# Row 0 of w3 and half of w_out loaded in fp32 on SP and cast on chip, q of batch 0 on POOL's queue, all queues listed anew

## The chip, the cores and the metric

The kernel runs on one core of one Trainium2 chip. The metric is device time in microseconds: the median of several executions. Five engines run their own instruction queues: TensorE (PE: matmuls and transposes; PEld is its loading of weights), VectorE (DVE), ScalarE (ACT), GpSimd (POOL) and SyncE (SP). Here POOL and SP also issue the transfers between memory and the chip; 16 DMA engines carry them. Transfers issued by POOL can change the type on the way (fp32 in memory, fp16 on chip); those that SP issues copy as they are.

## The reference, cut to what matters

```python
# q, k, v: (8, 8, 576, 64); w1, w2: (512, 1024); w3: (1024, 1024); w_out: (1024, 512), all fp32
q_s = softmax(q, over the 64 features); k_s = softmax(k, over the 576 positions)
kv  = einsum('bhsd,bhse->bhde', k_s, v)
x   = einsum('bhsd,bhde->bhse', q_s, kv)      # laid out as 4608 tokens x 512
h   = (x @ w1) * (x @ w2) @ w3
out = h @ w_out                               # 4608 x 512
```

## The kernel before, in words

The two last products are folded: W3O = w3 @ w_out is made once (1024 x 512), and each token needs only x @ w1, x @ w2, their product elementwise, and one product with W3O. All matmuls take fp16 operands.

The work is cut into named steps. A step's name holds its kind, batch or chunk, and part. A class `Plan` (L19 on) takes every step with its engine, what it needs and what it frees; the order in which the steps are emitted is not computed but written out in one long text, `ORDER`. Each engine gets its instructions in that order and runs them strictly one behind the other; semaphores make a step wait for what it needs. `PICKS` says which engine does a step that more than one engine could do (evictions from the matmul banks above all). The lists `HW`, `LOADS` and `LATE` give the transfers: `HW` and `LATE` go to SP's queue, `LOADS` to POOL's, each in the order of its list (L436 to L441). A load on POOL's queue also waits until the load eight before it has landed. `FILL` puts empty matmuls (L362, on a tile of zeros) into TensorE's queue at the start and ahead of a named step.

The steps that the prediction speaks of:

- `w3.r` loads rows of w3: r = 0 to 3 are one block of 128 rows each, `w3.4` holds blocks 4 and 5, `w3.5` blocks 6 and 7. `wo.0` and `wo.1` load the halves of w_out. `w1.c`, `w2.c` load a quarter of the columns of w1 and w2. `q.0.p`, `k.b`, `v.b` load q, k, v; q of batches 0 and 1 comes in two parts, p = 0 of 1024 and p = 1 of 1280 elements on each of 128 partitions.
- Folding, for each block ft of w3 (L453 to L484): `w3t.ft` transposes it on TensorE (eight 128x128 transposes, L457), `w3T.ft` copies it out on ACT or DVE, `pf.ft.0` and `pf.ft.1` multiply it with the two halves of w_out (four matmuls each, L469), `W3O.ft` copies the result out with a scale.
- q of batch b, part p: `qmx` (largest of 64, DVE, L640), `qsub` (DVE or POOL, L645), `qexp` (ACT, L653), `qsm` (sum, DVE, L658), `qeps`, `qrc` (reciprocal), `qn` (product, POOL, L677). For batch 0 `qt.0.n` then transposes it on TensorE (L692), and `qT` copies that out.
- k of batch 0: `kmx.0.0` (four operations on DVE, L510 to L513), `kT`, `kr`, `kB` (largest over all positions, by TensorE and DVE, L547 to L559), `ksub`, `kexp`; `kv.0` multiplies with v (L603, L613), `kv2` scales, `xm` and `xt` make x (L725).
- Chunk c of tokens: `up.1.c.s.u` is the product with w2, `up.0.c.s.u` that with w1 (L857), `bs` copies the first out, `ab` multiplies the two on DVE (L872), `down` is the product with W3O (L879, L894 for the last chunk), `os` copies it out and `st` stores it.

Before, `HW` is the two parts of q of batch 0, and `LOADS` begins with w3.4, w3.0, wo.0, wo.1, k.0, w3.3, w3.2, w3.5, v.0, k.1, q.1.0, w2.0, w1.0, w3.1, w2.1, w1.1. The fold starts with block 4.

Of the kernel before, what the change touches and what calls it, by code (L numbers as in the profile page):

```python
# [82 lines left out]
W3O.2 w3T.6 w3T.7 kve.0 k.2 pf.7.0 w2.2 pf.6.0 kv2.0 xm.0.0 w1.2 kmx.1.0 qmx.1.0 cba.1 xs.0.0.0 w2.3
qsub.1.0 xs.0.0.1 w1.3 pf.6.1 pf.7.1 xm.0.1 xs.0.1.1 xs.0.1.0 W3O.7 up.1.0.0.0 up.0.0.0.0 bs.0.0.0
cbx.1 ab.0.0.0 cb.1 xt.0 up.1.0.1.0 bs.0.1.0 W3O.6 v.1 w3t.1 w3T.1 ksub.1.1 q.1.1 up.0.0.1.0
up.1.0.0.1 ab.0.1.0 pf.1.0 up.0.0.0.1 qexp.1.0 xts.0.0 xts.0.1 bs.0.0.1 qsm.1.0 ab.0.0.1 up.1.0.1.1
up.0.0.1.1 pf.1.1 kexp.1.1 kmx.2.0 qeps.1.0 W3O.1 bs.0.1.1 up.1.0.0.2 up.0.0.0.2 up.1.0.1.2 qrc.1.0
ab.0.1.1 bs.0.0.2 cba.2 cbx.2 ab.0.0.2 up.0.0.1.2 bs.0.1.2 ab.0.1.2 ksub.1.0 q.2 up.1.0.0.3
up.0.0.0.3 up.1.0.1.3 up.0.0.1.3 cb.2 bs.0.0.3 kexp.1.0 qn.1.0 ksub.2.1 ab.0.0.3 down.0.0 ksub.2.0
vc.1.1 vc.1.0 qmx.1.1 os.0.0 bs.0.1.3 kv.1 kve.1 ab.0.1.3 kv2.1 qmx.2.1 qsub.1.1 down.0.1 down.0.2  # L90
qd.1.0 kexp.2.0 os.0.1 kexp.2.1 qexp.1.1 xm.1.0 down.0.3 xs.1.0.0 xs.1.0.1 qmx.2.0 qsub.2.1 qsub.2.0
qsm.1.1 qeps.1.1 os.0.2 qrc.1.1 qexp.2.1 qexp.2.0 qn.1.1 v.2 k.3 q.3 up.1.1.0.0 up.0.1.0.0 bs.1.0.0
up.1.1.0.1 up.0.1.0.1 ab.1.0.0 st.0.0 vc.2.0 bs.1.0.1 qd.1.1 qsm.2.1 qeps.2.1 os.0.3 ab.1.0.1 st.0.3
st.0.1 qrc.2.1 qn.2.1 qsm.2.0 qd.2.1 vc.2.1 qeps.2.0 up.1.1.0.2 up.0.1.0.2 up.1.1.0.3 up.0.1.0.3
qrc.2.0 qn.2.0 qd.2.0 bs.1.0.2 ab.1.0.2 bs.1.0.3 kv.2 kve.2 ab.1.0.3 down.1.0 kv2.2 qmx.3.1 xm.1.1
down.1.1 xs.1.1.0 xs.1.1.1 xt.1 os.1.0 kmx.3.0 xts.1.0 xts.1.1 cba.3 qmx.3.0 up.1.1.1.0 up.0.1.1.0
up.1.1.1.1 up.0.1.1.1 bs.1.1.0 qsub.3.1 qsub.3.0 bs.1.1.1 xm.2.0 cbx.3 ab.1.1.0 xs.2.0.0 cb.3
xs.2.0.1 qexp.3.1 up.1.1.1.2 up.0.1.1.2 xm.2.1 xs.2.1.1 bs.1.1.2 ab.1.1.1 ab.1.1.2 xs.2.1.0
up.1.1.1.3 up.0.1.1.3 up.1.2.0.0 bs.1.1.3 qsm.3.1 ksub.3.0 q.4 ab.1.1.3 bs.2.0.0 qexp.3.0 qmx.4.1
ksub.3.1 up.0.2.0.0 up.1.2.0.1 up.0.2.0.1 up.1.2.0.2 bs.2.0.1 ab.2.0.0 qsm.3.0 up.0.2.0.2 up.1.2.0.3  # L100
ab.2.0.1 up.0.2.0.3 kexp.3.0 qeps.3.0 qrc.3.0 qsub.4.1 bs.2.0.2 up.1.2.0.4 qeps.3.1 qn.3.0 kexp.3.1
ab.2.0.2 qrc.3.1 qn.3.1 st.0.2 k.4 v.4 v.3 q.5 vc.3.1 qmx.4.0 kmx.4.1 qsub.4.0 bs.2.0.3 down.1.2
up.0.2.0.4 vc.3.0 os.1.1 os.1.2 up.1.2.0.5 qexp.4.1 bs.2.0.4 bs.2.0.5 kv.3 ab.2.0.3 kmx.4.0 ab.2.0.4
down.1.3 qd.3.0 qmx.5.1 qd.3.1 qexp.4.0 os.1.3 kve.3 kv2.3 vc.4.1 vc.4.0 qsub.5.1 up.0.2.0.5
ab.2.0.5 up.1.2.0.6 up.0.2.0.6 xm.3.1 bs.2.0.6 xm.3.0 ab.2.0.6 xs.3.0.1 xs.3.1.0 xs.3.1.1 xs.3.0.0
xt.2 cba.4 qsm.4.0 cbx.4 up.1.2.0.7 up.0.2.0.7 bs.2.0.7 v.5 k.5 q.6 st.1.0 st.1.2 xts.2.0 qeps.4.0
up.1.3.0.0 up.0.3.0.0 cb.4 ab.2.0.7 bs.3.0.0 ab.3.0.0 xts.2.1 ksub.4.1 qsm.4.1 up.1.3.0.1 up.0.3.0.1
up.1.3.0.2 bs.3.0.1 up.0.3.0.2 up.1.3.0.3 ab.3.0.1 up.0.3.0.3 down.2.0 qeps.4.1 qmx.5.0 kmx.5.1
qrc.4.1 kexp.4.1 qexp.5.1 ksub.4.0 bs.3.0.2 kexp.4.0 qsub.5.0 qn.4.1 os.2.0 bs.3.0.3 vc.5.1 qexp.5.0
st.1.3 v.6 st.1.1 st.2.0 qd.4.1 kv.4 ab.3.0.2 kmx.5.0 up.1.3.0.4 up.0.3.0.4 qrc.4.0 qn.4.0 ab.3.0.3  # L110
up.1.3.0.5 up.0.3.0.5 qsm.5.1 qeps.5.1 cba.5 bs.3.0.4 vc.6.1 down.2.1 kve.4 qsm.5.0 vc.5.0 cbx.5
os.2.1 down.2.2 down.2.3 cb.5 ksub.5.0 bs.3.0.5 qd.4.0 ab.3.0.5 qrc.5.1 ab.3.0.4 up.1.3.0.6
up.0.3.0.6 kv2.4 os.2.2 os.2.3 qmx.6.1 bs.3.0.6 xm.4.1 xt.3 qeps.5.0 ab.3.0.6 qrc.5.0 xs.4.1.1
ksub.5.1 kexp.5.0 qn.5.0 xs.4.1.0 qmx.6.0 k.6 up.1.3.0.7 bs.3.0.7 up.0.3.0.7 ab.3.0.7 down.3.0
kmx.6.0 os.3.0 kmx.6.1 kexp.5.1 xts.3.0 xts.3.1 xm.4.0 xt.4 xts.4.1 kv.5 kve.5 xs.4.0.0 xts.4.0
xs.4.0.1 qn.5.1 cba.6 down.3.1 down.3.2 kv2.5 up.1.4.0.0 vc.6.0 bs.4.0.0 cbx.6 st.2.2 up.0.4.0.0
up.1.4.0.1 up.0.4.0.1 up.1.4.0.2 qd.5.0 st.2.1 qd.5.1 st.2.3 ab.4.0.0 qsub.6.1 bs.4.0.1 st.3.0 q.7
k.7 v.7 os.3.1 os.3.2 st.3.1 ab.4.0.1 cb.6 xm.5.1 xm.5.0 bs.4.0.2 xs.5.0.1 xs.5.0.0 xs.5.1.1
qexp.6.1 ksub.6.1 up.0.4.0.2 up.1.4.0.3 qsub.6.0 ab.4.0.2 up.0.4.0.3 up.1.4.0.4 bs.4.0.3 up.0.4.0.4
ksub.6.0 kexp.6.1 bs.4.0.4 qexp.6.0 xs.5.1.0 ab.4.0.3 up.1.4.0.5 ab.4.0.4 bs.4.0.5 up.0.4.0.5  # L120
up.1.4.0.6 qsm.6.1 ab.4.0.5 kexp.6.0 qeps.6.1 bs.4.0.6 up.0.4.0.6 up.1.4.0.7 qmx.7.1 up.0.4.0.7
up.1.5.0.0 bs.4.0.7 ab.4.0.7 qrc.6.1 ab.4.0.6 down.3.3 qn.6.1 down.4.0 vc.7.1 os.3.3 qsm.6.0
# [878 lines left out]
```

## Time and profile before

| | |
|---|---|
| median of 3 runs | 239.43 us (239.19 to 239.56) |
| the profiled execution | 239.15 us, its span 237.4 us |
| TensorE busy | 229.5 us, 97% of the span |
| VectorE busy | 172.7 us, 73% |
| ScalarE busy | 122.1 us, 51% |
| POOL busy | 115.5 us, 49% |
| moved by DMA | 46.84 MB, mean 197 GB/s |

The span runs from the first to the last instruction of the profile; some 1.75 us of the execution lie around it. Busy time does not tell what bounds a kernel. The prediction reads TensorE's idle time from its instructions in order of time, and what ended each wait. A row of a timeline has the start, the length, engine, line, operation, the tiles by name, and the count; in brackets stands the idle time before it and what ended it. Where several instructions of one kind follow each other they are one row, from the first start to the last end, so that rows of TensorE, whose matmuls are pipelined, overlap a little. Tile names: `w` is w3 on chip, `wosb` w_out, `w1sb` and `w2sb` the others, `en` the normalized q, `po` and `pab` matmul banks.

### The profile page before, as it was taken

To read this page: it belongs to the slowest core of one execution; us is meant where nothing else is said; L and a number is where in the kernel's file an instruction comes from. 1 tells how busy PE (TensorE), PEld (TensorE's weight loads), DVE (VectorE), ACT (ScalarE), POOL (GpSimd) and SP (SyncE) were. 2 spreads that over 40 slices of the span, in tenths; PEclk is the share of its full clock that TensorE was granted. 3 is DMA by queue.
4 is the path that set the end of the run, shared out by engine and by line. 5 is a ranking of instruction groups with operands and counts; after the bars stand their busy time and mean duration, and the time that the engine had idled before them with its cause. 6 is when DMAs were issued, how large, how long until landed. Compare 5 with 4: busy or idle time off the path is not lost.

```text
span 237.4 us, 4852 instructions
## 1 busy us (share of the span) xinstructions
PE 229.5 (97%) x1935; PEld 119.1 (50%) x1935; DVE 172.7 (73%) x263; ACT 122.1 (51%) x225; POOL 115.5 (49%) x75
## 2 busy tenths in 40 slices
...
GB/s 211 214 310 207 343 202 303 322 309 384 300 225 309 403 342 266 391 391 157 237 115 193 401 172 102 143 79 3 122 68 0 1 3 133 29 94 95 50 132 133
DMA packets 40038, 46.84 MB, mean 197 GB/s; under 512 B 18384, under 2 KB 24272, under 8 KB 40016
## 3 DMA queue, kind: packets, MB, share of 16 engines
...
q8 instruction: 15, 0.25, 0.4%
q14 instruction: 7, 0.06, 0.1%
...
## 4 chain that ended last, share of the span: by engine, by line
PE 90%; DMA 6%; DVE 1%; POOL 1%; issue 1%; ACT 0%; ACTq 0%; DVEq 0%; POOLq 0%
PE pab L857 53%; PE po L879 24%; DMA k<-in_k_dram 6%; PE po L469 4%; PE po L894 3%; PE pkv L603 2%; PE xm L725 1%; PE pab L725 1%; PE w3t L457 1%; PE po L725 1%; DVE kmx L510 1%; POOL wosb L416 0%; POOL w L416 0%; DVE kmx L511 0%; DVE w3T L335 0%
## 5 line engine op out<-in xcount | busy, mean ns | idle before, releaser
L872 DVE TENSOR_TENSOR ab<-pab,bsb 128x512 f16<-128x512 f32 x72 | 48.5, 682 | 29.8 <-PE pab L857 15.1
L857 PE MATMUL pab<-x,w2sb 128*128 128x512 f16 (+1 forms) x320 | 66.0, 337 | 0.0
L857 PE MATMUL pab<-x,w1sb 128*128 128x512 f16 (+1 forms) x320 | 65.9, 337 | 0.0
L879 PE MATMUL po<-W3O,ab 128*128 128x512 f16 x256 | 59.2, 379 | 0.0
L857 PEld LDWEIGHTS <-w1sb 128*128 128x128 f16 x352 | 34.0, 98 | 28.5 <-issue 0.8
L857 PEld LDWEIGHTS <-w2sb 128*128 128x128 f16 x352 | 33.6, 98 | 28.1 <-issue 1.1
L335 ACT CAST bsb<-pab 128x512 f16<-128x512 f32 x47 | 27.1, 586 | 27.2 <-PE pab L857 26.9
L677 POOL TENSOR_TENSOR en<-eq,qr 128x1280 f16<-128x1280 f16 (+1 forms) x15 | 32.8, 2196 | 17.0 <-ACT qr L664 10.0
L578 POOL TENSOR_TENSOR k<-k,cb 128x1152 f32<-128x1152 f32 x12 | 31.5, 2632 | 19.5 <-issue 10.0
L879 PEld LDWEIGHTS <-ab 128*128 128x128 f16 x256 | 24.5, 98 | 28.9 <-issue 0.4
L335 ACT COPY osb<-po 128x512 f32<-128x512 f32 (+1 forms) x26 | 14.9, 575 | 40.9 <-PE po L879 35.2
L645 POOL TENSOR_TENSOR q<-q,qm 128x1024 f32<-128x1024 f32 (+1 forms) x14 | 29.7, 2125 | 5.7 <-issue 4.0
L640 DVE TENSOR_REDUCE qm<-q 128x16 f32<-128x1024 f32 (+1 forms) x16 | 21.4, 1340 | 3.3 <-DMA q<-in_q_dram 3.3
L658 DVE TENSOR_REDUCE qr<-eq 128x20 f32<-128x1280 f16 (+1 forms) x16 | 21.4, 1336 | 1.7 <-ACT eq L653 1.7
L335 DVE CAST bsb<-pab 128x512 f16<-128x512 f32 x25 | 17.1, 683 | 7.6 <-PE pab L857 7.1
L586 ACT ACTIVATE ek<-k 128x1152 f16<-128x1152 f32 x16 | 18.6, 1163 | 6.9 <-DVE k L578 3.6
L653 ACT ACTIVATE eq<-q 128x1024 f16<-128x1024 f32 (+1 forms) x16 | 18.5, 1164 | 3.9 <-DVE q L645 3.0
L501 DVE TENSOR_REDUCE km<-k 128x128 f32<-128x1152 f32 x8 | 17.3, 2168 | 0.0
L469 PE MATMUL po<-wosb,w3T 128*128 128x512 f16 x64 | 15.5, 379 | 0.7 <-DMA wosb<-in_moe_w_out_dram 0.5
L335 DVE COPY osb<-po 128x512 f32<-128x512 f32 (+1 forms) x11 | 7.2, 664 | 5.9 <-PE po L894 5.6
L335 ACT CAST v<-v 128x1152 f16<-128x1152 f32 x9 | 10.3, 1156 | 1.8 <-DMA v<-in_v_dram 1.8
L469 PEld LDWEIGHTS <-w3T 128*128 128x128 f16 x64 | 5.8, 97 | 7.2 <-issue 0.9
...
## 6 DMA issues: line engine op xcount, KB each, us to landing
...
```

The lines of the kernel that those rows point to most:

```text
L335: return [(nc.scalar.copy if eng == "ACT" else engine[eng].tensor_copy)(out=out, in_=in_)]
L469: nc.tensor.matmul(st["pf", ft], lhsT=st["w3T", ft][:, gt, :], rhs=wosb[:, gt, :], start=(gt == 0), stop=(gt == N_FT - 1))
L578: return [engine[eng].tensor_tensor(out=kb[:, two(hp), :, :], in0=kb[:, two(hp), :, :], in1=st["cb", b][:, two(hp), None, :].broadcast_to( ...
L586: nc.scalar.activation(out=st["ek", b][:, hp, :, :].rearrange("p j (i d) -> p i j d", i=2), in_=kb[:, two(hp), :, :], func=AF.Exp)
L640: dve.tensor_reduce(out=st["qm", b][:, :, j], in_=qb[:, :, j, :], axis=AX.X, op=ALU.max)
L645: return [engine[eng].tensor_tensor(out=qb[:, :, j, :], in0=qb[:, :, j, :], in1=st["qm", b][:, :, j, None].broadcast_to([P, HH, n, D]), op ...
L653: nc.scalar.activation(out=st["eq", b, p], in_=qb[:, :, j, :], func=AF.Exp)
L658: dve.tensor_reduce(out=st["qr", b][:, :, slice(*PARTS[p])], in_=st["eq", b, p], axis=AX.X, op=ALU.add)
L677: return [engine[eng].tensor_tensor(out=st["en", b][:, j, :, :].rearrange("p j h d -> p h j d"), in0=st["eq", b, p], in1=st["qr", b][:, :, ...
L857: nc.tensor.matmul(st["p", one, c, sub, u][:, a * (t1 - t0):(a + 1) * (t1 - t0)], lhsT=w[:, ct, fb * P:(fb + 1) * P], rhs=x()[:, ct, t0:t1 ...
L872: dve.tensor_tensor(out=st["ab", c][:, nf * u:nf * u + nf, t0:t1], in0=cut(st["p", 0, c, sub, u]), in1=cut(st["bsb", c, sub, u]), op=ALU.mult)
L879: nc.tensor.matmul(st["po", c, tb], lhsT=st["ab", c][:, ft, tb * P:(tb + 1) * P], rhs=W3O[:, ft, :], start=(ft == 0), stop=(ft == N_FT - 1))
```

## The change

- `HW` becomes w3.0 and wo.1: SP loads the first block of w3 (512 KB) and the second half of w_out (1 MB) in fp32, into the buffers that q and v of batch 1 take later. New steps cast them to fp16, in pieces of 1024 elements for each partition: `cast.w3.0.0` and `cast.wo.1.0` on ACT, `cast.wo.1.1024` on VectorE. `w3t.0` needs the first, `pf.ft.1` the other two.
- Both parts of q of batch 0 move to the head of `LOADS`, on POOL's queue, the larger part first, then wo.0, w3.4, k.0, w3.3, w3.2, w3.1, w3.5, v.0, k.1, q.1.0, w2.0, w1.0, w1.1, w2.1. POOL makes the identity (`ident`) ahead of its first load.
- The fold starts with block 0. `FILL` goes from 17 fills at the start and 6 ahead of `pf.4.0` to 10 at the start and 16 ahead of `pf.0.0`.
- `ORDER`, `PICKS` and `LATE` are listed anew through the whole kernel. In batch 0, `qsub.0.0` goes from VectorE to POOL, `w3t.1` comes ahead of `kv.0` instead of between the first products of chunk 0, and `qt.0.0` stands right behind `kB.0`.

```diff
 ORDER = """
-q.0.0 qmx.0.0 qsub.0.0 qexp.0.0 q.0.1 qmx.0.1 w3.4 qsub.0.1 w3.0 wo.0 ident w3t.4 wo.1 k.0 qexp.0.1
-w3T.4 qsm.0.1 w3.3 w3.2 w3.5 v.0 w3t.0 w3t.5 w3T.0 qeps.0.1 qrc.0.1 ident32 pf.4.0 pf.0.0 pf.4.1
+w3.0 wo.1 ident cast.w3.0.0 w3t.0 w3T.0 cast.wo.1.1024 q.0.1 q.0.0 cast.wo.1.0 wo.0 w3.4 k.0 qmx.0.1
+qsub.0.1 w3.3 qmx.0.0 w3.2 pf.0.0 pf.0.1 w3t.5 qexp.0.1 ident32 qsm.0.1 qeps.0.1 qrc.0.1 w3.1 w3.5
+qsub.0.0 v.0 qn.0.1 k.1 qexp.0.0 w3t.4 w3T.5 pf.5.0 pf.5.1 w3T.4 W3O.0 qsm.0.0 qeps.0.0 qrc.0.0
+pf.4.0 pf.4.1 kmx.0.0 w3t.3 qt.0.16 W3O.5 w3T.3 q.1.0 w2.0 w1.0 w1.1 qn.0.0 w3t.2 qt.0.8 w2.1 W3O.4
+w3T.2 kT.0 kr.0 pf.3.0 kB.0 qT.0.16 qT.0.8 qt.0.0 qT.0.0 pf.2.0 pf.3.1 pf.2.1 w3t.6 w3t.1 w3t.7
...
 FILL = {
-    "begin": 17, "pf.4.0": 6,
+    "begin": 10, "pf.0.0": 16,
 }
...
 HW = [
-    ("q", 0, 0), ("q", 0, 1),
+    ("w3", 0), ("wo", 1),
 ]
...
 LOADS = [
-    ("w3", 4), ("w3", 0), ("wo", 0), ("wo", 1), ("k", 0), ("w3", 3), ("w3", 2), ("w3", 5), ("v",
-    0), ("k", 1), ("q", 1, 0), ("w2", 0), ("w1", 0), ("w3", 1), ("w2", 1), ("w1", 1), ("k", 2),
-    ("w2", 2), ("w1", 2), ("w2", 3), ("w1", 3), ("v", 1), ("q", 1, 1),
+    ("q", 0, 1), ("q", 0, 0), ("wo", 0), ("w3", 4), ("k", 0), ("w3", 3), ("w3", 2), ("w3", 1),
+    ("w3", 5), ("v", 0), ("k", 1), ("q", 1, 0), ("w2", 0), ("w1", 0), ("w1", 1), ("w2", 1),
+    ("k", 2), ("w2", 2), ("w1", 2), ("w2", 3), ("w1", 3), ("v", 1), ("q", 1, 1),
 ]
...
     def home(name):
-        x = RAW.index(name)
-        return [("v", 1), ("q", 1)][x // 2], slice(x % 2 * 1024, x % 2 * 1024 + 1024)
+        return {"wo": ("v", 1), "w3": ("q", 1)}[name[0]], 2048 if name[0] == "wo" else 1024
...
+    def pieces(name):
+        return [(x, x + 1024) for x in range(0, home(name)[1], 1024)]
+
+    def wt(n):
+        return [("cast", *n, x0) for x0, _ in pieces(n)] if n in RAW else [n]
...
     for name in RAW:
-        def cast(eng, name=name):
-            to = st["cast", name].rearrange("p a x -> p (a x)")
-            return copy(eng, to, raw(name))
-        plan.add(("cast", *name), {"DVE": (1.2, True), "ACT": (1.02, False)}, 0,
-                 cast, needs=[name], lead=60.0)
-    wt = lambda n: [("cast", *n) if n in RAW else n]
+        for x0, x1 in pieces(name):
+            def cast(eng, name=name, x0=x0, x1=x1):
+                to = st["cast", name].rearrange("p a x -> p (a x)")
+                return copy(eng, to[:, x0:x1], raw(name)[:, x0:x1])
+            plan.add(("cast", *name, x0), {"DVE": (1.2, True), "ACT": (1.02, False), "POOL": (1.15, True)}, 0,
+                     cast, needs=[name], lead=60.0)
```

More of the change, by code (lines that the diff above doesn't have):

```diff
@@ L83 @@
[L83 to L122, printed above, removed]
@@ new lines @@
+up.1.0.0.0 up.0.0.0.0 up.1.0.1.0 bs.0.0.0 cba.1 ab.0.0.0 bs.0.1.0 w2.3 w1.3 xt.0 up.0.0.1.0
+up.1.0.0.1 qsub.1.0 v.1 cbx.1 cb.1 up.0.0.0.1 ab.0.1.0 xts.0.1 qexp.1.0 qsm.1.0 bs.0.0.1 qeps.1.0
+q.1.1 ksub.1.1 pf.1.0 ab.0.0.1 W3O.6 kmx.2.0 qrc.1.0 kexp.1.1 up.1.0.1.1 pf.1.1 xts.0.0 bs.0.1.1
+W3O.1 cba.2 q.2 up.0.0.1.1 up.1.0.0.2 up.0.0.0.2 up.1.0.1.2 bs.0.0.2 ab.0.1.1 ab.0.0.2 bs.0.1.2
+ksub.1.0 cbx.2 cb.2 qn.1.0 qd.1.0 up.0.0.1.2 up.1.0.0.3 ab.0.1.2 up.0.0.0.3 up.1.0.1.3 up.0.0.1.3
+kexp.1.0 vc.1.1 vc.1.0 bs.0.0.3 ab.0.0.3 down.0.0 ksub.2.1 bs.0.1.3 kv.1 qmx.1.1 qsub.1.1 ab.0.1.3
@@ new lines @@
+os.0.0 down.0.1 down.0.2 kexp.2.1 kve.1 kv2.1 qmx.2.1 qexp.1.1 os.0.1 os.0.2 xm.1.0 xs.1.0.1
+ksub.2.0 xs.1.0.0 qsub.2.1 down.0.3 up.1.1.0.0 up.0.1.0.0 up.1.1.0.1 qmx.2.0 qsm.1.1 qsub.2.0
+qeps.1.1 qrc.1.1 qexp.2.1 qsm.2.1 qn.1.1 k.3 v.2 q.3 vc.2.0 bs.1.0.0 ab.1.0.0 bs.1.0.1 up.0.1.0.1
+up.1.1.0.2 up.0.1.0.2 up.1.1.0.3 qd.1.1 st.0.0 st.0.2 qexp.2.0 ab.1.0.1 kexp.2.0 qeps.2.1 qrc.2.1
+qsm.2.0 qn.2.1 qd.2.1 vc.2.1 bs.1.0.2 kv.2 qeps.2.0 ab.1.0.2 bs.1.0.3 up.0.1.0.3 qrc.2.0 qn.2.0
+ab.1.0.3 kve.2 os.0.3 kv2.2 qmx.3.1 down.1.0 kmx.3.0 cba.3 xm.1.1 xs.1.1.0 xs.1.1.1 qsub.3.1 qd.2.0
@@ new lines @@
+qmx.3.0 q.4 st.0.1 down.1.1 xt.1 up.1.1.1.0 up.0.1.1.0 os.1.0 os.1.1 xts.1.1 up.1.1.1.1 bs.1.1.0
+up.0.1.1.1 xts.1.0 ab.1.1.0 xm.2.0 cbx.3 xs.2.0.0 cb.3 xs.2.0.1 bs.1.1.1 qexp.3.1 ab.1.1.1
+up.1.1.1.2 up.0.1.1.2 bs.1.1.2 xm.2.1 up.1.1.1.3 up.0.1.1.3 xs.2.1.0 xs.2.1.1 ab.1.1.2 bs.1.1.3
+qsm.3.1 qsub.3.0 qexp.3.0 ksub.3.0 up.1.2.0.0 ksub.3.1 up.0.2.0.0 up.1.2.0.1 qsm.3.0 qeps.3.1
+qrc.3.1 qn.3.1 qeps.3.0 ab.1.1.3 qrc.3.0 qn.3.0 k.4 st.0.3 v.3 q.5 qd.3.1 bs.2.0.0 vc.3.1 kexp.3.1
+ab.2.0.0 kmx.4.0 bs.2.0.1 down.1.2 up.0.2.0.1 up.1.2.0.2 qmx.4.1 bs.2.0.2 kexp.3.0 os.1.2 up.0.2.0.2
@@ new lines @@
+up.0.3.0.7 bs.3.0.7 ab.3.0.7 down.3.0 qrc.5.0 k.6 st.2.1 down.3.1 kmx.6.1 kmx.6.0 v.6 cba.6 qd.5.1
+xs.4.0.0 xs.4.0.1 kexp.5.0 kexp.5.1 qn.5.0 os.3.0 qd.5.0 st.2.3 st.3.0 xt.4 kv.5 xts.4.0 xts.4.1
+cbx.6 vc.6.0 q.7 qmx.6.1 up.1.4.0.0 up.0.4.0.0 kve.5 bs.4.0.0 down.3.2 ab.4.0.0 kv2.5 qmx.6.0
+up.1.4.0.1 up.0.4.0.1 up.1.4.0.2 bs.4.0.1 os.3.1 st.3.1 v.7 st.2.2 os.3.2 ab.4.0.1 bs.4.0.2
+up.0.4.0.2 up.1.4.0.3 ab.4.0.2 bs.4.0.3 xm.5.1 xm.5.0 xs.5.1.1 xs.5.0.0 xs.5.0.1 xs.5.1.0 up.0.4.0.3
+up.1.4.0.4 up.0.4.0.4 up.1.4.0.5 ab.4.0.3 bs.4.0.4 up.0.4.0.5 up.1.4.0.6 ab.4.0.4 up.0.4.0.6 cb.6
@@ new lines @@
+qsub.6.1 qexp.6.1 qsub.6.0 vc.6.1 down.3.3 qsm.6.1 bs.4.0.5 qexp.6.0 qeps.6.1 ab.4.0.5 qmx.7.1
+ksub.6.0 bs.4.0.6 qsm.6.0 up.1.4.0.7 up.0.4.0.7 ab.4.0.6 bs.4.0.7 up.1.5.0.0 up.0.5.0.0 qeps.6.0
+ab.4.0.7 bs.5.0.0 up.1.5.0.1 up.0.5.0.1 qrc.6.1 qmx.7.0 ksub.6.1 kexp.6.1 kexp.6.0 qrc.6.0 ab.5.0.0
+up.1.5.0.2 up.0.5.0.2 k.7 kmx.7.1 bs.5.0.1 down.4.0 up.1.5.0.3 kv.6 qn.6.0 qsub.7.1 bs.5.0.2 st.3.2
+qd.6.0 qn.6.1 kmx.7.0 cba.7 ab.5.0.1 up.0.5.0.3 vc.7.1 qexp.7.1 os.3.3 os.4.0 cbx.7 vc.7.0 qd.6.1
+st.4.0 down.4.1 up.1.5.0.4 ab.5.0.2 bs.5.0.3 down.4.2 st.3.3 ab.5.0.3 cb.7 os.4.1 bs.5.0.4
```

79 lines of the change are left out of this document (46 added, 33 removed), and 111 rows, old and new, of the table PICKS.

## The prediction

> **What bounds the kernel now.** I read the stretches first, to learn where TensorE is not busy, then TensorE's instructions in order of time in the first 15 us, then the chain that ended last, and then the queues that feed those microseconds. The stretches (start:end, length, then busy microseconds of each engine with instruction counts, PE, PEld, DVE, ACT, POOL, then clock, DMA share and GB/s):
>
> ```profile
> 23.00:234.40 211.40, 211.31 (x1826) 109.99 (x1824) 158.60 (x241) 113.02 (x212) 100.53 (x53) 1.00 0.72 194
> 60.00:120.00 60.00, 59.94 (x576) 32.35 (x573) 55.50 (x82) 45.68 (x89) 50.14 (x26) 1.00 0.99 295
> ```
>
> From 23 us to its last matmul TensorE is busy 211.31 of 211.40 us. There is 0.1 us to win there, whatever is listed anew; there is more to lose, since VectorE is busy 55.50 of 60 us in the middle. So the time is decided by how much of its work TensorE has done by about 34 us. The start, in order of time (start, length, then what; in brackets the idle time before it):
>
> ```profile
> 1.55 5.66 PE L362 MATMUL po<-zero 128*128 128x512 f16 x17 [1.55 <-DVE zero L357]
> 8.64 0.70 PE L457 MATMUL w3t<-ident,w 128*128 128x128 f16 x8 [1.43 <-DMA w<-in_moe_w_dram]
> 9.93 1.20 PE L457 MATMUL w3t<-ident,w 128*128 128x128 f16 x16 [0.59 <-DMA w<-in_moe_w_dram]
> 10.97 1.46 PE L362 MATMUL po<-zero 128*128 128x512 f16 x6
> 12.48 1.89 PE L469 MATMUL po<-wosb,w3T 128*128 128x512 f16 x8
> 14.82 0.38 PE L469 MATMUL po<-wosb,w3T 128*128 128x512 f16 x1 [0.46 <-DMA wosb<-in_moe_w_out_dram]
> ```
>
> Here every step but the empty fills (L362) waits for a transfer. The landings are those of one stream: w3 rows 4 and 5 at 8.64, row 0 at about 9.9, the first half of w_out by 12.4, the second at 14.8. In source bytes, 2.62 MB in 6.18 us is 0.424 MB/us. Later, the chain that ended last (start, length, what):
>
> ```profile
> 22.42 0.59 PE kB L559 x8
> 23.01 0.65 PE w3t L457 x8
> 23.66 0.86 PE po L469 x4
> 24.52 0.45 PE qtp L692 x8
> 24.97 1.73 PE po L469 x8
> 26.69 0.49 PE w3t L457 x8
> 27.19 0.71 PE pkv L603 x72
> 27.89 0.54 PE pkv L613 x36
> 28.43 1.83 PE po L469 x8
> 30.26 0.34 PE xm L725 x8
> 30.60 1.83 PE po L469 x8
> 32.44 0.34 PE xm L725 x8
> 32.78 1.33 PE pab L857 x11
> ```
>
> TensorE is dense here. The first products with w2 start at 32.78, those with w1 eight matmuls later, at about 33.65. The queues (packets, MB, share of the engines, in the slice from 5 to 6 us; then single issues of 256 KB with their time to landing), and POOL's issues in order of time:
>
> ```profile
> q1 hardware_dynamic: 196, 0.23, 68.1%
> q0 software_dynamic: 47, 0.10, 50.7%
> ...
> w1sb<-in_moe_w_dram POOLq DMA_DIRECT2D x1, 256.0 KB, 15.5
> ...
> w<-in_moe_w_dram POOLq DMA_DIRECT2D x1, 256.0 KB, 15.5
> ```
> ```profile
> 13.46 2.34 POOL L677 TENSOR_TENSOR en<-eq,qr 128x1280 f16<-128x1280 f16 x1 [2.54 <-DVE qr L670]
> 15.75 0.81 POOL L416 DMA_DIRECT2D q<-in_q_dram  x1
> 16.55 0.76 POOL L416 DMA_DIRECT2D w2sb<-in_moe_w_dram  x1
> 18.05 0.74 POOL L416 DMA_DIRECT2D w1sb<-in_moe_w_dram  x1 [0.74 <-DMA k<-in_k_dram]
> 19.18 0.54 POOL L416 DMA_DIRECT2D w<-in_moe_w_dram  x1 [0.39 <-DMA w<-in_moe_w_dram]
> 20.42 0.74 POOL L416 DMA_DIRECT2D w2sb<-in_moe_w_dram  x1 [0.69 <-DMA w<-in_moe_w_dram]
> 21.18 1.92 POOL L677 TENSOR_TENSOR en<-eq,qr 128x1024 f16<-128x1024 f16 x1
> ```
>
> The first piece of w1, issued at 18.05, lands 15.5 us later, at 33.55, 0.1 us before its use. Row 1 of w3, queued behind it, lands at 19.18 + 15.5 = 34.68: 0.52 MB of source take 1.13 us. So the stream and TensorE finish the start together.
>
> **The change, part by part.** The bytes read do not change: fp32 is read from memory either way, and a casting transfer only writes half. So I order the transfers by source bytes and give each the landing of before at the same count.
>
> Weights on SP, q on POOL. SP's queue now carries 0.52 MB of w3 and 1.05 MB of w_out where it carried 1.18 MB of q. POOL makes the identity before its first transfer, about 0.65 us later than now; POOL's packets begin only in the slice from 5 to 6 us above, as SP's run out, so SP's 0.39 MB more cover that. If they did not, the whole stream would slip by up to 0.65 us. Row 0 of w3 lands as the first 0.52 MB of q do now. These rows are VectorE's (and one of ScalarE's):
>
> ```profile
> 4.56 1.22 DVE L640 TENSOR_REDUCE qm<-q 128x16 f32<-128x1024 f32 x1 [3.06 <-DMA q<-in_q_dram]
> 5.81 1.23 DVE L645 TENSOR_TENSOR q<-q,qm 128x1024 f32<-128x1024 f32 x1
> 6.95 1.48 DVE L640 TENSOR_REDUCE qm<-q 128x20 f32<-128x1280 f32 x1
> 8.46 1.49 DVE L645 TENSOR_TENSOR q<-q,qm 128x1280 f32<-128x1280 f32 x1
> 11.29 1.49 DVE L658 TENSOR_REDUCE qr<-eq 128x20 f32<-128x1280 f16 x1 [1.34 <-ACT eq L653]
> ```
> ```profile
> 9.99 1.27 ACT L653 ACTIVATE eq<-q 128x1280 f16<-128x1280 f32 x1 [1.86 <-DVE q L645]
> ```
>
> So row 0 is there at 4.56. ScalarE casts it in about 1 us (by its 1.27 us for 1280 elements), and TensorE transposes it at about 5.75, behind the ten fills that are left, 4 us sooner than now. That gains nothing: the next product, row 0 with w_out, needs the first half of w_out, which is third on POOL's queue. With 3.80 MB up to its end, as now, it lands at about 12.4. The 16 fills run from 6.3 to about 10 and cost nothing, because that wait covers them to 12.4. The other two casts (1 us on ScalarE, and 1.2 to 1.5 us on VectorE by the rows above) start when w_out's second half lands, at about 7.2; VectorE is done by 8.7, and then q arrives. Without that cover VectorE's cast would delay q by its own length.
>
> TensorE to 23 us. First product at 12.45, eight matmuls, 14.2. Rows 4 and 5 of w3 come at 4.85 MB, where w_out's second half was: 14.85. Sixteen transposes take 1.04 (9.93 to 10.97 above): 15.9. The copy of the first of them on VectorE ends at about 16.25, so 0.35 idle. From there to the end of kB stands the same work as now after 14.82: sixteen matmuls 3.46, two sets of transposes 1.04, ten of q 0.55, kT 0.44, four matmuls 0.87, kB 0.6, together 6.96. End at 23.2; now it is 22.42 + 0.59 = 23.0.
>
> q's chain. q's larger part lands at 2.23 MB, where rows 4 and 5 of w3 were: 8.65, about 2.4 us later than now. VectorE reduces it (1.48) and subtracts (1.49): 11.65; it reduces the smaller part (1.22): 12.85. The smaller subtraction moves to POOL: 1.92 by the row for that size, 14.75. Behind it wait, on POOL, the issue of v (0.77; its bytes are due only after 23 us, so no loss), the larger product (2.34; ScalarE 1.27, VectorE 1.49 and two small steps make its input ready at 15.1): 17.85; then five issues, 0.8 + 4 x 0.76, 21.7; then the smaller product (1.92): 23.6, against 23.1 now. Its transposes now stand right behind kB: 23.65, so 0.4 idle on TensorE. Their 0.45, twelve matmuls 2.6, and three sets of transposes 1.5 give 28.2; kv 1.25, eight matmuls 1.73, xm 0.34, eight matmuls 1.73, xm 0.34: the first product with w2 at 33.6. One of those three sets is row 1 of w3, which now comes after 33.65 and takes 0.49. On TensorE alone the change costs 33.6 - 32.78 - 0.49 = 0.33 us.
>
> The stream. Row 1 of w3 now goes ahead of the pieces of w1 and w2. So the first piece of w1 lands where row 1 did, at 34.68, and its product starts at 34.74 instead of 33.65; TensorE waits 0.27 us for it, behind 33.6 + 0.87. Less the 0.49 us done early: **+0.60 us**. The two costs are not added, since the wait contains the first.
>
> Bounds of the stream. The 1.57 MB on SP can move as q did there (1.18 MB by about 5.6 us, 0.39 MB/us) or as the weights do now (0.424): 0 to 0.3 us later; the 1.18 MB of q, now on POOL, may gain by the same two rates, up to 0.25 us. I take 0, between them; the ends are +0.35 and +0.9.
>
> The rest. The list moves about as many evictions to VectorE as from it and reorders later loads and stores. I cost it at nothing: the cover is that 211.31 of 211.40 us. If it fails, one reduction of 1.2 to 1.5 us ahead of a multiply on VectorE is the price each time.
>
> Sum: the profiled execution took 239.15 us, span 237.4. Plus 0.60 is 239.75. The median of the runs, 239.43, lies 0.28 higher; against it I forecast **240.0 us**, with 239.8 to 240.4 for this case alone.
>
> **The rivals.** About 0.2%, 0.48 us, is what a measurement of this kernel can tell from no change.
>
> *Nothing to measure.* The weights need no cast in the transfer, and the stream runs some 0.3 us earlier. Then w1 comes with TensorE's own path, and +0.3 is left: 239.7. For it: q's gain may be near its 0.25; against it: casting transfers read faster now than SP's q did, and less of them is left. That the change does not do what it says belongs here: the early fold of row 0 moves one transpose, and nothing behind it.
>
> *The array's clock drops.* The 17 fills take 5.66 us where eight matmuls of L469 take 1.73, so 17 should take 3.68: a slow start costs up to 1.98 us. After the fills TensorE is idle from about 10 to 12.4. If it starts slowly again there, the first eight matmuls end at 15.9 instead of 14.2, 1.05 beyond the wait that follows, and 0.25 falls behind it; the 0.4 us of q's wait vanish. The first product with w1 starts at 35.4: +1.3, 240.7. Against it: in the rows above there is no untransposed matmul from 7.21 to 10.97, and the six fills then take 1.46, which is 0.24 each.
>
> [...]
>
> *A new wait in the relisted rest*, with VectorE the bound between 60 and 120 us: +0.6 + 1.5, 241.5. For it: 55.50 of 60 busy; against it: the present list has the same load and no wait.
>
> *Faster.* The large rows of the fp32 weights move on SP so much faster that the stream leads by over 1.08 us; then both bounds lie below now, 0.33 - 1.08 on TensorE and 0.60 - 1.08 by w1; the later decides, -0.48: 238.95 and below. For the first 2.75 MB that needs 0.57 MB/us on SP, against 0.39 to 0.424 in any row above.
>
> **How the numbers follow.** Forecast 0.46, nothing to measure 0.26, clock 0.08, new wait 0.11, faster 0.09. The forecast's lower edge, 239.8, lies within 0.48 us of 239.43, so 0.06 of it counts as the same. Faster 0.09; same 0.26 + 0.06 = 0.32; slower 0.40 + 0.08 + 0.11 = 0.59. The range runs from 239.2, which leaves out faster, to 241.1, which takes in the clock and leaves out most of the new wait.
>
> **What would show it.** In the profile after: the transposes of row 0 near 5.75 us, the first product at 12.4 waiting for w_out, rows 4 and 5 at 14.85; transposes of q at 23.6 behind POOL's product; the first product with w1 near 34.7 with a wait for its transfer; no TensorE wait later, the last matmul near 235.0. First products of 0.43 us each would show the clock. A landing of w1 well before 34 us, or a TensorE wait after 36 us, would make the prediction wrong.

## The result and the profile after

The changed kernel takes **240.11 us** (median of 6 runs, 239.76 to 240.49), the kernel before 239.25 us beside it (239.00 to 239.56): a ratio of 1.0036, with a 95% interval from 1.0023 to 1.0049. The profiled execution took 240.19 us, its span 238.4 us.

First TensorE's instructions in order of time after the change (start, length, then what; in brackets the idle time before it):

```profile
1.55 4.45 PE L363 MATMUL po<-zero 128*128 128x512 f16 x10 [1.55 <-DVE zero L358]
5.79 0.72 PE L463 MATMUL w3t<-ident,w 128*128 128x128 f16 x8
6.35 3.62 PE L363 MATMUL po<-zero 128*128 128x512 f16 x16
12.56 3.40 PE L475 MATMUL po<-wosb,w3T 128*128 128x512 f16 x8 [2.60 <-DMA wosb<-in_moe_w_out_dram]
15.76 1.33 PE L463 MATMUL w3t<-ident,w 128*128 128x128 f16 x16
17.38 3.63 PE L475 MATMUL po<-wosb,w3T 128*128 128x512 f16 x16 [0.29 <-DVE w3T L336]
...
24.16 0.62 PE L698 MATMUL qtp<-ident,en 128*128 128x128 f16 x8
...
34.35 1.05 PE L863 MATMUL pab<-x,w2sb 128*128 128x256 f16 x8
35.23 1.04 PE L863 MATMUL pab<-x,w1sb 128*128 128x256 f16 x8
```

Row 0 of w3 is transposed at 5.79 and the first product starts at 12.56, as forecast. But its eight matmuls take 3.40 us, 0.43 each, where sixteen at 17.38 take 3.63. The transposes of rows 4 and 5 do not wait for their transfer any more; they wait for TensorE. The same stretch by time (start:end, length, busy time of PE, PEld, DVE, ACT, POOL, then the granted clock, DMA share, GB/s), and two stretches that cover the rest:

```profile
12.00:12.50 0.50, 0.00 (x0) 0.00 (x0) 0.50 (x1) 0.50 (x1) 0.00 (x0) 1.00 1.06 201
12.50:13.00 0.50, 0.44 (x2) 0.27 (x3) 0.36 (x1) 0.50 (x2) 0.06 (x1) 0.77 1.10 209
13.00:16.00 3.00, 3.00 (x10) 1.17 (x9) 1.76 (x2) 1.58 (x4) 2.98 (x3) 0.50 1.07 342
16.00:16.50 0.50, 0.50 (x10) 0.50 (x9) 0.00 (x0) 0.00 (x0) 0.50 (x1) 0.82 1.01 415
...
23.00:34.00 11.00, 11.00 (x187) 6.39 (x185) 8.09 (x13) 7.52 (x13) 5.20 (x7) 1.00 1.21 278
34.00:235.40 201.40, 201.31 (x1649) 103.98 (x1648) 150.94 (x230) 105.48 (x203) 96.04 (x48) 1.00 0.69 188
```

The clock is granted at half from 12.77 to 16.18 us (0.77 and 0.82 are means over half a microsecond; 0.46 and 0.36 of those slices at half). That is 3.41 us. It drops 2.8 us after the last fill ended at 9.97, and 0.21 us after the first product has begun; those 0.21 are all the work of TensorE in the 2.8. The record of the clock does not show the slow start: it stands at 1.00 from 1.5 us on, where the first ten fills take 4.45 us, 0.44 each. So a mean below 1 in what follows counts later drops alone. From 17.4 us on TensorE waits for nothing, so no wait after the start costs time.

Two more rows, the transfer of the first piece of w1 (the last number is the time from issue to landing; issued at 20.18) and POOL's smaller product of q:

```profile
w1sb<-in_moe_w_dram POOLq DMA_DIRECT2D x1, 256.0 KB, 14.9
```
```profile
20.18 1.53 POOL L422 DMA_DIRECT2D w1sb<-in_moe_w_dram  x2
21.99 1.90 POOL L683 TENSOR_TENSOR en<-eq,qr 128x1024 f16<-128x1024 f16 x1 [0.28 <-DVE km L519]
```

The piece lands at about 35.1, 0.15 before its product. POOL's product ends at 23.89, 0.27 before q's transposes at 24.16. So three things stand close together: TensorE slowed by the clock, q's chain, and the stream. The experiments try them one by one.

### The profile page after: what moved, and what is told of

Same layout as the page of the kernel before. It is cut to its first block, busy times and chain, and to the rows that moved or that the text cites. A ratio compares the mean times of both kernels' runs of the same rounds, so it can differ in the third digit from the quotient of the medians.

```text
span 238.4 us, 4874 instructions
## 1 busy us (share of the span) xinstructions
PE 230.9 (97%) x1938; PEld 119.8 (50%) x1938; DVE 172.3 (72%) x262; ACT 123.3 (52%) x227; POOL 117.7 (49%) x77
## 4 chain that ended last, share of the span: by engine, by line
PE 93%; DMA 4%; POOL 1%; DVE 0%; issue 0%; ACT 0%; POOLq 0%; ACTq 0%
PE pab L863 53%; PE po L885 23%; PE po L475 7%; DMA wosb<-in_moe_w_out_dram 4%; PE po L900 3%; PE pkv L609 2%; PE w3t L463 1%; PE pab L731 1%; PE xm L731 1%; POOL q L422 1%; PE po L731 1%; PE qtp L698 0%; DVE w3T L336 0%; PE kB L565 0%; PE xt L731 0%
## 5 line engine op out<-in xcount | busy, mean ns | idle before, releaser
L336 ACT CAST bsb<-pab 128x512 f16<-128x512 f32 x48 | 27.9, 583 | 47.0 <-PE pab L863 47.0
L584 POOL TENSOR_TENSOR k<-k,cb 128x1152 f32<-128x1152 f32 x13 | 34.1, 2632 | 13.2 <-DVE km L519 6.2
L683 POOL TENSOR_TENSOR en<-eq,qr 128x1280 f16<-128x1280 f16 (+1 forms) x15 | 32.0, 2143 | 12.1 <-DVE qr L676 11.8
L651 POOL TENSOR_TENSOR q<-q,qm 128x1024 f32<-128x1024 f32 (+1 forms) x13 | 27.3, 2107 | 17.3 <-DVE qm L646 12.3
L336 ACT COPY osb<-po 128x512 f32<-128x512 f32 (+1 forms) x29 | 16.5, 578 | 27.6 <-PE po L885 22.7
L646 DVE TENSOR_REDUCE qm<-q 128x20 f32<-128x1280 f32 (+1 forms) x16 | 21.3, 1340 | 0.8 <-DMA q<-in_q_dram 0.8
L659 ACT ACTIVATE eq<-q 128x1280 f16<-128x1280 f32 (+1 forms) x16 | 18.6, 1163 | 5.2 <-DVE q L651 3.5
L475 PE MATMUL po<-wosb,w3T 128*128 128x512 f16 x64 | 16.7, 408 | 2.9 <-DMA wosb<-in_moe_w_out_dram 2.6
L336 DVE COPY osb<-po 128x512 f32<-128x512 f32 (+1 forms) x8 | 5.3, 661 | 10.0 <-PE po L900 5.7
L363 PE MATMUL po<-zero 128*128 128x512 f16 x26 | 8.1, 476 | 1.6 <-DVE zero L358 1.6
```

The source lines that it names most:

```text
L336: return [(nc.scalar.copy if eng == "ACT" else engine[eng].tensor_copy)(out=out, in_=in_)]
L475: nc.tensor.matmul(st["pf", ft], lhsT=st["w3T", ft][:, gt, :], rhs=wosb[:, gt, :], start=(gt == 0), stop=(gt == N_FT - 1))
L584: return [engine[eng].tensor_tensor(out=kb[:, two(hp), :, :], in0=kb[:, two(hp), :, :], in1=st["cb", b][:, two(hp), None, :].broadcast_to( ...
L646: dve.tensor_reduce(out=st["qm", b][:, :, j], in_=qb[:, :, j, :], axis=AX.X, op=ALU.max)
L651: return [engine[eng].tensor_tensor(out=qb[:, :, j, :], in0=qb[:, :, j, :], in1=st["qm", b][:, :, j, None].broadcast_to([P, HH, n, D]), op ...
L659: nc.scalar.activation(out=st["eq", b, p], in_=qb[:, :, j, :], func=AF.Exp)
```

## The experiments

Theory 1: the half clock alone costs the time. Theory 2: the order of the stream (row 1 of w3 ahead of w1) has the same price and lies just beneath it. A third floor, q's chain, came out of the first runs. This table holds what follows from the traces: how much later than before the first product with w1 starts (33.61 in the trace of before; 0.49 is taken off where row 1 of w3 is transposed ahead of it), how much later the last matmul ends (234.39 before), and the difference of the medians. The first two columns are of one profiled execution each. The rows of before, and the end of the changed kernel (start, length; the last two from the chain that ended last):

```profile
33.61 1.05 PE L857 MATMUL pab<-x,w1sb 128*128 128x256 f16 x8
...
227.45 6.94 PE po L894 x40
```
```profile
228.38 6.94 PE po L900 x40
```

| kernel | first product with w1 | last matmul | median |
|---|---|---|---|
| changed kernel | +1.13 | +0.93 | +0.86, again +1.10 |
| no fills ahead of pf.0.0 | +2.03 | +1.89 | +1.98 |
| 27 fills | +1.01 | +0.88 | +0.62 |
| 20 fills | +0.78 | +0.63 | +0.53 |
| 27 fills, qn.0.0 early | +0.44 | +0.49 | +0.46 |
| before, row 1 early | +1.07 | +0.77 | +0.66 |

A shift at the start comes out at the end to within 0.3 us.

**The changed kernel again.**

> The changed kernel itself, beside the next two on one chip: 240.1, eight first products in 3.40 us at half clock.

240.36 us (239.64 to 240.98), ratio 1.0048 (1.0033 to 1.0064). Of its six runs one had a mean granted clock of 1.000 and took 239.64; the other five had 0.991 to 0.993 and took 240.16 to 240.98. The same program without the drop, if only once, was 0.52 us faster than the fastest of these with it (of the first six, all at 0.992 or 0.993, the fastest took 239.76). In the profile TensorE is idle for 2.50 us, and the clock drops at 12.91 (0.91 in the slice), 0.38 us after the product has begun:

```profile
12.53 3.24 PE L475 MATMUL po<-wosb,w3T 128*128 128x512 f16 x8 [2.50 <-DMA wosb<-in_moe_w_out_dram]
```
```profile
12.50:13.00 0.50, 0.47 (x2) 0.22 (x3) 0.33 (x1) 0.50 (x2) 0.09 (x1) 0.91 1.17 221
```

**More fills, so that TensorE does not idle.**

```diff
-    "begin": 10, "pf.0.0": 16,
+    "begin": 10, "pf.0.0": 27,
```

> Only the count of empty fills ahead of pf.0.0 is raised, 16 to 27, so that TensorE has no idle time of 2.6 us before the first product. Both theories expect the eight matmuls of pf.0.0 at 0.21 to 0.24 us each (1.7 to 1.9 us together instead of 3.40), done by about 14.3, and the granted clock at 1.00 throughout. Theory 1, the clock alone costs the 0.9 us: the last matmul ends some 0.9 us earlier, 239.2. Theory 2, the order of the stream has the same price and lies just beneath: TensorE is early, but then waits 0.7 to 0.9 us for the first piece of w1, which still lands at about 35.05; gain 0.2 to 0.3 us, 239.9.

239.83 us, ratio 1.0026 (1.0015 to 1.0037). TensorE in order of time:

```profile
12.88 1.89 PE L475 MATMUL po<-wosb,w3T 128*128 128x512 f16 x8 [0.24 <-DMA wosb<-in_moe_w_out_dram]
15.24 1.21 PE L463 MATMUL w3t<-ident,w 128*128 128x128 f16 x16 [0.47 <-DMA w<-in_moe_w_dram]
16.74 3.63 PE L475 MATMUL po<-wosb,w3T 128*128 128x512 f16 x16 [0.30 <-DVE w3T L336]
...
24.01 0.62 PE L698 MATMUL qtp<-ident,en 128*128 128x128 f16 x8 [0.42 <-ACT qT L336]
...
34.23 1.05 PE L863 MATMUL pab<-x,w2sb 128*128 128x256 f16 x8
35.11 1.04 PE L863 MATMUL pab<-x,w1sb 128*128 128x256 f16 x8
```

The clock stays up (1.000 in the profile), the eight matmuls take 1.89, and after a wait for rows 4 and 5 the next sixteen start at 16.74, 0.64 sooner than in the changed kernel. But only 0.12 of it reaches the first product with w2. Most of the gain is lost at 24.01: q's transposes wait 0.42 us. The row names ScalarE, whose copy of the q transposed before ends at 24.01; but in the changed kernel such transposes start at 24.16 while that copy runs to 24.66, so they need not wait for it. POOL's product ends at 23.95:

```profile
21.97 1.98 POOL L683 TENSOR_TENSOR en<-eq,qr 128x1024 f16<-128x1024 f16 x1
```

Theory 1 falls as it stood. Against the kernel before, the loss goes from 0.86 and 1.10 us to 0.62, so the clock alone gives back 0.2 to 0.5 us, not 0.9; the profiled execution, the slowest of its seven, shows 0.05 at the last matmul. Theory 2 has the size right and the place wrong: the wait is q's, 10 us before w1 is wanted.

**No fills ahead of the first product.**

```diff
-    "begin": 10, "pf.0.0": 16,
+    "begin": 10,
```

> The 16 fills ahead of pf.0.0 are left out; the ten at the start stay. If these fills, which end 2.6 us too early, buy nothing, the first product still runs at half clock from 12.5 and the time is that of the changed kernel, 240.1 (within 0.2). If they do shorten the slow time (idle of 2.6 instead of about 6 us), the product takes longer than 3.40 us or more work runs at the half clock, and the time is up to 0.5 longer, 240.6.

241.19 us, ratio 1.0083 (1.0070 to 1.0097): the 16 fills, though they end too early, are worth 0.9 to 1.1 us, about twice the 0.5 at most that was expected. TensorE, and the clock by stretches:

```profile
12.77 3.57 PE L475 MATMUL po<-wosb,w3T 128*128 128x512 f16 x8 [6.73 <-DMA wosb<-in_moe_w_out_dram]
```
```profile
8.00:8.50 0.50, 0.00 (x0) 0.00 (x0) 0.00 (x0) 0.10 (x1) 0.00 (x0) 0.88 1.06 371
8.50:18.00 9.50, 5.23 (x25) 2.84 (x25) 6.64 (x7) 2.81 (x4) 5.75 (x5) 0.50 1.07 286
18.00:18.50 0.50, 0.50 (x3) 0.22 (x3) 0.50 (x1) 0.42 (x1) 0.50 (x1) 0.50 1.09 201
18.50:19.00 0.50, 0.50 (x4) 0.19 (x3) 0.50 (x1) 0.50 (x2) 0.50 (x2) 0.88 1.15 217
```

Half clock from 8.38 to 18.62, 10.24 us. That is three times the 3.41 us of the changed kernel: although TensorE works from 12.77 on, the clock comes back only after 5.9 us of work, against 3.6 in the changed kernel (12.56 to 16.18). What sets these lengths is not shown.

**Twenty fills.**

```diff
-    "begin": 10, "pf.0.0": 16,
+    "begin": 10, "pf.0.0": 20,
```

> 20 fills ahead of pf.0.0 instead of 16: they end near 10.9, and TensorE is idle for some 1.7 us instead of 2.6. If an idle time of that length leaves the clock up, the first eight matmuls take 1.7 to 1.9 us and the time is that of the run with 27 fills, 239.8; if any idle time there drops it, they take 3.4 and the time stays at 240.1.

239.85 us, ratio 1.0024 (1.0015 to 1.0033), as with 27.

```profile
12.79 1.89 PE L475 MATMUL po<-wosb,w3T 128*128 128x512 f16 x8 [2.40 <-DMA wosb<-in_moe_w_out_dram]
```

The fills ran faster at the start (3.86 us for the first ten instead of 4.45), so the idle time was 2.40, not the 1.7 expected. Still the clock stayed up, here and in all ten runs (mean 0.999 or 1.000). In the profiles with 16 fills ahead of the first product it dropped, with idle times of 2.50 and 2.60 us in the changed kernel and 2.81 with row 1 late. The other nine runs need not have had 2.40 us: a slower start, as in the changed kernel, ends the fills later. Whether the shorter idle time kept the clock up in the profile, or its place in time, is open.

**The smaller product of q earlier on POOL.** With 27 fills, and:

```diff
-q.1.0 w2.0 w1.0 w1.1 qn.0.0 w3t.2
+q.1.0 w2.0 w1.0 qn.0.0 w1.1 w3t.2
```

> 27 fills, and on POOL the smaller product of q (qn.0.0) ahead of the issue of w1.1 instead of behind it, so that it ends at 23.2 instead of 23.9. New theory: three floors lie within 0.3 us of each other, the clock, q's chain and the landing of w1. With the first two lifted, the transposes of q follow kB without the 0.42 us of idle time, the first product with w2 starts at 33.8 instead of 34.23, and then TensorE waits 0.3 to 0.4 us for the first piece of w1, which lands at about 35.05: 239.7, a gain of 0.1 or less over 27 fills alone. If the landing of w1 is no floor, the whole 0.42 comes back, 239.4.

239.78 us, ratio 1.0018 (1.0009 to 1.0027).

```profile
23.36 0.62 PE L695 MATMUL qtp<-ident,en 128*128 128x128 f16 x8
...
33.56 1.05 PE L860 MATMUL pab<-x,w2sb 128*128 128x256 f16 x8
34.54 1.05 PE L860 MATMUL pab<-x,w1sb 128*128 128x256 f16 x8
```
```profile
w1sb<-in_moe_w_dram POOLq DMA_DIRECT2D x1, 256.0 KB, 14.1
```

The wait at q's transposes is gone, and the first product with w2 comes 0.67 earlier than with 27 fills alone (0.16 of it is there before, at the products that start at 16.58 instead of 16.74). The next starts 0.98 later instead of 0.88: it stands for 0.1 us behind the landing of w1, issued at 20.36, so at 34.46. That is the third floor, 0.6 below where I had put it. Why the piece lands sooner here is not shown: behind the same issues ahead of it, it landed at 34.7 to 35.1 in the kernels that issue w1.1 right after it. The last matmul ends 0.44 earlier than in the changed kernel; the time still lies above before.

**The stream's part alone, in the kernel before.** Row 1 of w3 loaded ahead of w2 and w1, nothing else:

```diff
-    0), ("k", 1), ("q", 1, 0), ("w2", 0), ("w1", 0), ("w3", 1), ("w2", 1), ("w1", 1), ("k", 2),
+    0), ("k", 1), ("q", 1, 0), ("w3", 1), ("w2", 0), ("w1", 0), ("w2", 1), ("w1", 1), ("k", 2),
```

> The kernel before with one part of the change alone: row 1 of w3 is loaded ahead of the first pieces of w2 and w1 instead of behind them; its transposes stay where they are. The prediction's step on the stream expects the first piece of w1 at 34.7 and its product there instead of 33.65, with a wait of about 1.0 us: 240.3. If the first piece of w1 isn't delayed by the whole transfer (in the runs of the changed kernel it landed anywhere from 34.5 to 35.1 as its neighbours in the queue moved), the wait is shorter: 239.3 to 240.0.

The list of issues in `ORDER` follows. 239.92 us, ratio 1.0032 (1.0020 to 1.0044), +0.66.

```profile
33.54 1.05 PE L853 MATMUL pab<-x,w2sb 128*128 128x256 f16 x8 [0.67 <-DMA w2sb<-in_moe_w_dram]
34.68 1.05 PE L853 MATMUL pab<-x,w1sb 128*128 128x256 f16 x8
```
```profile
19.29 0.74 POOL L412 DMA_DIRECT2D w1sb<-in_moe_w_dram  x1 [0.41 <-DMA w<-in_moe_w_dram]
...
w1sb<-in_moe_w_dram POOLq DMA_DIRECT2D x1, 256.0 KB, 15.4
```

19.29 + 15.4 is 34.69, and the product starts at 34.68: the landing that the prediction worked out. Most of TensorE's wait, 0.67 us, stands ahead of that, at the piece of w2, which is pushed back too. Of the 1.07 us by which it comes later, 0.77 reach the last matmul; where the other 0.3 went, no row shows, and the time stays 0.4 below the 240.3 expected for the full wait.

**Row 1 of w3 late, in the changed kernel.** Loaded behind w1.0, transposed behind `xt.0`, its copy (`w3T.1`, on ScalarE) right behind that:

```diff
-pf.2.1 w3t.6 w3t.1 w3t.7
+pf.2.1 w3t.6 w3t.7
...
-qmx.1.0 w3T.1 xm.0.1
+qmx.1.0 xm.0.1
...
-xt.0 up.0.0.1.0
+xt.0 w3t.1 w3T.1 up.0.0.1.0
```

> Row 1 of w3 is loaded behind the first piece of w1 and transposed after the transposition of x, as before; the fills stay. The first piece of w1 lands about 1.1 us earlier, at 33.9. Theory 1, the clock: TensorE has no wait to lose, only the 0.49 us of transposes change place: 240.1, no change. If instead the order of the stream were the whole cost and the clock hidden, 239.3.

243.48 us, ratio 1.0160 (1.0140 to 1.0181): neither theory. ScalarE, VectorE and TensorE, in this order:

```profile
37.68 1.01 ACT L331 COPY w3T<-w3t 128x1024 f16<-128x1024 f16 x1 [1.99 <-PE w3t L458]
38.72 0.82 ACT L529 COPY mx<-mx 32x8 f32<-32x8 f32 x4
...
39.57 0.17 DVE L535 TENSOR_REDUCE mxe<-mx 128x8 f32<-128x16 f32 x1 [2.03 <-ACT mx L529]
...
48.40 1.03 PE L858 MATMUL pab<-x,w2sb 128*128 128x256 f16 x8 [1.07 <-DVE ab L873]
```

ScalarE waits 1.99 us for the late transposes, and the maxima of k of batch 1 queue behind the copy; VectorE waits 2.03 us for those; 9 us later TensorE waits 1.07 for a multiply on VectorE. That is a third of the 3.4 us by which this span is longer than the changed kernel's; 0.74 is a wait at 95.76, 0.9 a longer last store, and the rest was not traced. With 27 fills beside it (243.48 becomes 242.42, ratio 1.0135) the wait at 48 us is the same:

> Both edits together: 27 fills, and row 1 of w3 behind the first piece of w1. Theory 1 expects no more than from the fills alone, 239.2. Theory 2, two bounds of the same size: only here the whole comes back, the first product with w2 at about 33.1, last matmul 0.8 to 1.0 us earlier than in the changed kernel, 239.1 to 239.3, while each edit alone gave 0.3 or less.

So these two say nothing on the two theories. Repeated with qn.0.0 early, 27 fills, and the copy two steps further back on ScalarE, behind the copy of the transposed x:

```diff
-xt.0 w3t.1 w3T.1 up.0.0.1.0
+xt.0 w3t.1 up.0.0.1.0
...
-ab.0.1.0 xts.0.1 qexp.1.0
+ab.0.1.0 xts.0.1 w3T.1 qexp.1.0
```

> 27 fills, the smaller product of q ahead of the issue of w1.1, and row 1 of w3 loaded behind the first piece of w1 and transposed behind the transposition of x. Unlike the first try with a late row 1, its copy on ScalarE stands behind the copy of the transposed x and not ahead of what k of batch 1 needs. If that place in ScalarE's queue cost the 3.4 us there, TensorE has no wait near 48 us now. The transposes only change place, so the first product with w2 comes 0.49 earlier, at about 33.1, and the time is that of the run with qn early, 239.7 to 239.8; below 239.5 if the landing of w1 still held it up. If the late row 1 itself cost the time, 241 or more.

The wait at 48 us is gone, so that place in ScalarE's queue did cost it. The first product with w1 starts at 34.19, the last matmul ends at 235.15, 0.17 before the changed kernel's. But the time is 240.56, ratio 1.0054 (1.0042 to 1.0066). Its span is 0.8 us longer than that of the kernel with qn.0.0 early; 0.27 of it is there at the last matmul, and some 0.5 lies behind it, at the last store (first this kernel, then the one with qn.0.0 early; KB, us to landing):

```profile
out_dram<-osb SPq DMA_DIRECT2D x1, 96.0 KB, 2.3
```
```profile
out_dram<-osb SPq DMA_DIRECT2D x1, 96.0 KB, 1.6
```

The last store took 2.3 to 2.5 us in the three kernels with row 1 late, and 1.6 in the others whose profile has it. Why is open.

**The first part of q of batch 1 behind w1**, with 27 fills and qn.0.0 early:

```diff
-    ("w3", 5), ("v", 0), ("k", 1), ("q", 1, 0), ("w2", 0), ("w1", 0), ("w1", 1), ("w2", 1),
+    ("w3", 5), ("v", 0), ("k", 1), ("w2", 0), ("w1", 0), ("q", 1, 0), ("w1", 1), ("w2", 1),
```

In `ORDER` the issue follows, and the first reduction of that part (`qmx.1.0`, on VectorE) goes back behind `cba.1`.

> As the run before, and the first part of q of batch 1 (0.52 MB of source) is loaded behind the first piece of w1 instead of ahead of w2 and w1; its first reduction on VectorE goes behind the maxima of k of batch 1. The first piece of w1 then lands at about 33.9. Three floors lifted: no wait of TensorE before 36 us, first product with w1 at 34.7, 239.4, 0.7 under the changed kernel. If the batch-1 chain of q takes offence at 1.2 us of delay, a wait of TensorE after 45 us shows it, and the time is 0.5 to 1.5 longer.

240.24 us, ratio 1.0035 (1.0022 to 1.0049). The first product with w1 comes at 34.22, without a wait; the gain is given back soon:

```profile
37.61 1.05 PE L858 MATMUL pab<-x,w2sb 128*128 128x256 f16 x8 [0.32 <-DMA w2sb<-in_moe_w_dram]
...
46.85 1.03 PE L858 MATMUL pab<-x,w2sb 128*128 128x256 f16 x8 [0.35 <-DVE ab L873]
```

TensorE waits for the next piece of w2, then for a multiply on VectorE behind the chain of batch 1.

**The kernel before without its six fills.**

```diff
-    "begin": 17, "pf.4.0": 6,
+    "begin": 17,
```

> The kernel before without its six fills ahead of pf.4.0. TensorE then does only 24 transposes between 7.2 and 12.5 us, with idle pieces of about 1.4, 0.6 and 1.4 us. If transposes count as activity, or short pieces of idle time don't drop the clock, the first product still takes 0.21 to 0.24 us a matmul and the time is that of before, 239.2. If the clock drops, eight matmuls take 3.4 us instead of 1.9 and the time is 1.0 to 1.7 longer, 240.3 to 240.9.

239.29 us, ratio 1.0000 (0.9991 to 1.0009).

```profile
9.00 0.71 PE L457 MATMUL w3t<-ident,w 128*128 128x128 f16 x8 [0.86 <-DMA w<-in_moe_w_dram]
10.32 1.20 PE L457 MATMUL w3t<-ident,w 128*128 128x128 f16 x16 [0.61 <-DMA w<-in_moe_w_dram]
12.75 1.89 PE L469 MATMUL po<-wosb,w3T 128*128 128x512 f16 x8 [1.24 <-DMA wosb<-in_moe_w_out_dram]
```

4.6 us hold only 24 transposes, and the first product runs at full speed. In three of its ten runs the mean clock was 0.993, at 239.27 to 239.60, no longer than the rest. So here the clock is up in seven of ten runs with 1.9 us of transposes in that gap, and the change emptied the gap. Whether the transposes keep it up is not shown. And a drop need not cost time: in these three runs none shows, while in the changed kernel, whose eight first products take 3.40 us, it does.

## Why the prediction was right, and where it was not

The time was right (240.0 forecast, 240.11 and 240.36 measured, both within the range), and slower was the likeliest outcome. One step that carries it was not. That the number came out is luck in part: +0.57 us was forecast, +0.86 and +1.10 were found, and 0.2 of the difference is hidden because the kernel before came out lower, at 239.25, than the 239.43 that the forecast stands on.

- *Only the start matters; the relisted rest at nothing.* Right: 201.31 of 201.40 us busy after 34 us. The rival of a new wait there did not come true in the changed kernel. Such waits came when I altered the list by hand (row 1 late, q of batch 1 late), at 0.3 to 1.1 us each.
- *Row 0 at 4.56, cast, transposed at 5.75.* 5.79. VectorE's cast of w_out was put at 1.2 to 1.5 us by the fp32 rows. It takes 0.69:

```profile
7.27 0.69 DVE L336 CAST wosb<-v 128x1024 f16<-128x1024 f32 x1
8.72 1.49 DVE L646 TENSOR_REDUCE qm<-q 128x20 f32<-128x1280 f32 x1 [0.76 <-DMA q<-in_q_dram]
```

  The reduction of 128x1024 in the same trace takes 1.21, so here it did not price the cast of as many elements. The cast stayed hidden.
- *"The 16 fills run from 6.3 to about 10 and cost nothing, because that wait covers them to 12.4."* **This is the step that failed.** The fills ended at 9.97 as said, but what matters is what follows an idle time of 2.6 us: eight matmuls in 3.40 instead of 1.73. The rival for just this, "the array's clock drops", worked it out closely (first eight done at 15.9, found 15.96; first product with w1 at 35.4, found 35.23; q's wait gone, as found), and I gave it 0.08. Its sign, first products of 0.43 us, appeared; that of the forecast, a wait of the first product with w1, did not. The row against it (six fills at 0.24 each after a gap) was of a gap with 24 transposes in it. In two traces the clock fell 2.3 us after TensorE's last work (6.04 to 8.38, no fills) and 2.8 us after the last fill (9.97 to 12.77). In the two traces of the changed kernel the drop came in the midst of work, 0.21 and 0.38 us into the product. How much idle time, and where, is needed for a drop, no run here settles; in the kernel before without its six fills, with 24 transposes in a gap of 4.6 us, the mean clock was 1.000 in seven of ten runs.
- *q's chain.* Right: 23.6 forecast for its end on POOL, 23.89 found (0.28 of it a wait that the row at 21.99 puts down to k's maxima), and the 0.4 us wait that goes with it showed as 0.42 as soon as the clock was mended. In the changed kernel TensorE was late itself.
- *The stream: w1 lands at 34.68 and its product waits.* Right alone, to 0.01 us, when this part was put into the kernel before; that run costs 0.66. In the changed kernel the piece landed at about 35.1, 0.4 later than forecast, where the bounds allowed 0.3; why is open. TensorE came to it at 35.23 on its own account, so this was not what decided.
- *The two costs are not added.* Right, and the reason why the time came out near with the wrong step in it. Three floors stand within about 0.7 us: the clock, q's chain, the landing of w1. Lifting the first gave 0.2 to 0.5 us by the medians; lifting the second gave another 0.16 by the medians and 0.39 at the last matmul of the profiles, and then the third showed. A forecast that sees one of three nearly equal floors can be right in time and wrong in cause, and that is what happened here.
- *Nothing to measure, or faster.* Not found: both intervals of the changed kernel lie above 1.002. The 0.57 MB/us that "faster" asks for does not come out of its own numbers: 1.57 MB take 3.70 us at 0.424, and 1.08 less makes 0.60. It changes no step.
